# Fewer score products and paced dummies in the first four attention pairs, and units 16 to 23 computed by pairs

## The chip, the cores and the metric

The kernel runs on one core of a Trainium2 chip. The metric is the device time of one execution in microseconds (us): the median of several runs of the same program. The engines are TensorE (PE; its weight loads stand apart as PEld), VectorE (DVE), ScalarE (ACT), GpSimd (POOL) and SyncE (SP), which here only issues DMA transfers. Each engine works through its own instructions in order, and waits on semaphores for what the others make.

## The reference, cut to what matters

q, k and v are float32; the weights come as 8-byte floats, whose words the kernel converts. First an attention over 2 batches, 8 heads, 768 positions and 64 dimensions, then two feed-forward stages over 1536 tokens:

```
k_sum = k.reshape(B, H, nb, 32, D).max(axis=3)      # 24 blocks of 32 keys
v_sum = v.reshape(B, H, nb, 32, D).mean(axis=3)
scores_l = scale * q @ k.T, kept where |i - j| < 16
scores_s = scale * q @ k_sum.T + log(32)
a = softmax(concat(scores_l, scores_s))
x = a @ concat(v, v_sum)                             # to 1536 x 512
x = ((x @ w_a) * (x @ w_b)) @ w_out                  # d_ff 1536
h = x @ w_in;  out = (h - tanh(h)) @ w_out2          # d_ff 2048
```

## The kernel before, in words

**Attention.** A unit is 64 query positions of one batch; there are 24, and units 2m and 2m+1 make pair m. A unit sees a window of 96 keys (KW) and the 24 block maxima, so it has 120 score columns (NK). All products of the attention are float32, which PE runs in two passes, so that one product shows as two records. Heads go by two: p counts four couples (NP), h is the head in the couple and picks 64 of the 128 partitions.

A pair's steps are: T1, four transposes of q (`T1t`) and their copy out of PSUM (`T1e`); T2, the score products (`T2m`), then on DVE the masked scores with their maximum (`tt`), on ACT the exponentials with their sum (`ex`), on DVE the reciprocal of the sum (`rb`) and the scaling (`nm`); T3, transposes of the weights (`T3t`) and their copy (`T3e`); T4, the products with v (`T4m`), whose high half ACT writes to X (`T4h`) and whose low half DVE subtracts (`T4l`). `W` copies the 96 keys of a unit beside its 24 maxima; `q_of`, `kw_of` and `vw_of` name the buffers.

`T2m` (line 252) works on products of 64 by 64: for each p, h and unit n one. For pairs 4 and up the keys lie beside their maxima, and one product makes all 120 columns. For pairs 0 to 3 the keys are read where they are, so there are two products, one of 96 and one of 24 columns: 32 products for such a pair.

**The feed-forward stages** take tokens in three blocks of 512. Their work is a list of positions (`pos`, line 505): for each f a projection with w_a, one with w_b (`pos_a`, `pos_b`, 12 products each) and one with w_out (`pos_o`, 12 products into four accumulators). Values and weights are split into a high and a low part in fp32r, hence three products for each. Positions 0 to 35 are block 0, 36 to 70 block 1, then comes block 2, which needs X of units 16 to 23, and from about 380 us on the second stage (`pos_h`, `pos_o2`).

**The order.** Up to position 35 it is written out by hand: the list `SEQ` (line 857) names every operation in order, on all engines, under manual scheduling (line 858). Its operations go by name and number: `T2m2` is the score products of pair 2, `Mp0_0` the first products of position 0, `L` something is a load, `da` to `df` convert weights, `KP` transposes keys of batch 1, `va` adds halves of v on POOL, `vm` is the mean of v over blocks on PE (line 776), `vme` its copy by ACT (line 780), `vc` copies of it into the v buffers of the units. `tt`, `ex`, `rb`, `nm` and `T3` count halves of pairs, 2m + h. `Zu` calls `single` (line 295): two memsets and four selects on POOL that prepare masks and a zeroed q buffer for units 16 to 23.

PE gets dummies in the head. `FILL` (line 623) puts plain transposes before an operation. `PACED` (line 625) puts groups before one: each is a product that reads a softmax sum, `SM[u]` (so PE waits there until that sum is done), and six transposes that nobody reads:

```
SM, PACED = {}, {'T1t4': [0, 3, 2, 6, 5], 'T2m2': [1], 'T3t1': [4], 'T3t6': [7]}
```

From position 36 on a planner (`plan`, line 546) puts operations ahead of positions, and the framework's scheduler orders all engines but SP from position 36 to 71, by priority; what runs under `high_priority` counts as 200 instructions earlier. There units 16 to 23 are computed one by one, one every four positions: `unit_T1` (line 302) writes the q of a pair block-diagonally, so that a unit's two heads share a product, `unit_T2m` (line 314) makes four products of 128 by 128 a unit, `unit_T3` four transposes, `unit_T4` eight products. A unit's chain from T1 to T4 is up to seven positions long, so the chains of neighbours overlap. All of them run under raised priority (line 594), PE's part too. `load_q` and `load_v` are issued by SP.

Of the kernel before, what the change touches and what calls it, by code (L numbers as in the profile page):

```python
# [39 lines left out]
def band_attention_moe_kernel(ctx: ExitStack, tc: tile.TileContext, q, k, v, w_a, w_b, w_out, w_in, w_out2, out):  # L40
# [873 lines left out]
```

## Time and profile before

| | |
|---|---|
| median of 3 runs | 646.63 us (645.88 to 648.36) |
| the profiled execution | 646.71 us |
| its span, first to last instruction | 644.8 us |
| mean granted clock of TensorE | 0.997 of full |
| first projection (position 0) | 47.51 us |
| PE busy | 633.3 us, 98% |
| DVE, ACT, POOL busy | 493.6, 471.4, 194.7 us |

The profile is of one execution. Times in rows count from the first instruction of the span. A timeline row gives the start, the busy time, the engine, the line of the kernel, the operation, what it writes and reads, and in brackets how long the engine was idle before it and what ended that. The chain of waits follows the work that ended last back to the start: each piece released the next. "issue" is time in which an engine waited for nothing that the profile shows. A window row gives for one stretch the busy time of each engine with the number of its instructions, the share of TensorE's full clock that was granted, the share of DMA and its rate.

### The profile page before, as it was taken

The numbers are of one execution on the slowest core, as the hardware profiler recorded it, in microseconds if no ns is written. First come the engines' busy times: TensorE is split into PE (matmuls) and PEld (weight loads), VectorE is DVE, ScalarE is ACT, GpSimd is POOL, SyncE is SP. The second block draws the span as 40 slices with busy tenths as digits, with TensorE's granted clock in tenths as the row PEclk, the third lists the DMA queues.
The fourth block names the chain that finished last, engine by engine and source line by source line (L and its number), as shares of the span: only waits on it lengthen the run. The fifth ranks groups of instructions, "written<-read, shape, count | busy, mean of one in ns | idle before, by whom it ended". The sixth has DMA issues, their size and how long they took to land.

```text
span 644.8 us, 10213 instructions
## 1 busy us (share of the span) xinstructions
PE 633.3 (98%) x3562; PEld 516.9 (80%) x3562; DVE 493.6 (77%) x995; ACT 471.4 (73%) x994; POOL 194.7 (30%) x207
## 2 busy tenths in 40 slices
PE   7889999999999999999999999999999999999997
PEld 5578888788888887888888888888888888888885
DVE  4799999899868666458877748877777877777775
ACT  4879999997778766356555458777777777777774
POOL 3551331111101010001111144544445554444441
PEclk9899999999999999999999999999999999999999
DMA  9989997662733553023445000000010000100001
GB/s 201 274 210 265 261 232 214 190 179 71 220 111 111 170 147 100 14 101 99 146 147 163 17 1 2 0 2 1 0 67 0 2 0 1 61 6 1 1 1 65
DMA packets 81679, 62.15 MB, mean 96 GB/s; under 512 B 45716, under 2 KB 72340, under 8 KB 81628
## 3 DMA queue, kind: packets, MB, share of 16 engines
q1 hardware_dynamic: 79276, 60.32, 33.5%
q0 software_dynamic: 2352, 1.18, 1.5%
q8 instruction: 28, 0.46, 0.3%
q14 instruction: 23, 0.19, 0.1%
HBM read 54.00 MB, written 7.34 MB: 95 GB/s over the span
## 4 chain that ended last, share of the span: by engine, by line
PE 96%; DVE 1%; DMA 1%; SPq 1%; issue 0%; ACT 0%; DVEq 0%; ACTq 0%
PE acc L485 20%; PE pa L396 15%; PE pb L396 15%; PE acc L424 10%; PE acc L831 5%; PE pb L837 5%; PE pa L837 5%; PE ps L396 5%; PE pt L396 5%; PE ps L318 1%; DMA XB<-in_k_dram 1%; PE ps L366 1%; PE pt L272 1%; SPq L642 1%; PE ps L631 1%; PE pt L356 1%
## 5 line engine op out<-in xcount | busy, mean ns | idle before, releaser
L185 POOL TENSOR_TENSOR wsp<-w,wsp 128x512 fp32r<-128x512 f32 x97 | 127.7, 1335 | 139.8 <-ACT wsp L184 139.8
L184 ACT ACTIVATE wsp<-w 128x512 fp32r<-128x512 f32 x165 | 98.8, 621 | 13.4 <-PE acc L424 9.4
L179 POOL TENSOR_SCALAR w<-w 128x512 f32<-128x512 f32 x39 | 26.5, 682 | 185.7 <-ACT w L154 97.3
L485 PE MATMUL acc<-wsp,gh 128*128 128x512 f32 x256 | 78.9, 389 | 0.0
L185 DVE TENSOR_TENSOR wsp<-w,wsp 128x512 fp32r<-128x512 f32 x68 | 48.4, 713 | 36.5 <-ACT wsp L184 36.2
L424 PE MATMUL acc<-gh,wsp 128*128 128x512 f32 x192 | 63.5, 391 | 0.0
L396 PE MATMUL pb<-XB,wsp 128*128 128x512 f32 x240 | 60.5, 394 | 0.0
L396 PE MATMUL pa<-XB,wsp 128*128 128x512 f32 x240 | 60.0, 394 | 0.0
L389 ACT ACTIVATE gh<-tg 128x512 fp32r<-128x512 f32 x56 | 34.9, 623 | 30.0 <-DVE tg L412 29.7
L485 PEld LDWEIGHTS acc<-wsp,gh 128*128 128x128 f32 x256 | 48.1, 188 | 10.0
L396 PEld LDWEIGHTS pa<-XB,wsp 128*128 128x128 f32 x240 | 44.5, 188 | 9.5
L396 PEld LDWEIGHTS pb<-XB,wsp 128*128 128x128 f32 x240 | 44.4, 188 | 9.1
L485 PE MATMUL acc<-wsp,gl 128*128 128x512 f32 x128 | 49.8, 389 | 0.0
L485 PE MATMUL acc<-wsp,vw 128*128 128x512 f32 x192 | 46.5, 390 | 0.0
L396 PE MATMUL pa<-XA,wsp 128*128 128x512 f32 x192 | 46.1, 389 | 0.0
L396 PE MATMUL pb<-XA,wsp 128*128 128x512 f32 x192 | 46.1, 389 | 0.0
L390 DVE TENSOR_TENSOR gl<-tg,gh 128x512 fp32r<-128x512 f32 x56 | 38.5, 687 | 8.8 <-ACT gh L389 8.8
L485 PEld LDWEIGHTS acc<-wsp,vw 128*128 128x128 f32 x192 | 35.9, 188 | 8.2 <-ACT vw L389 0.4
L396 PEld LDWEIGHTS pb<-XA,wsp 128*128 128x128 f32 x192 | 36.0, 188 | 7.5
L396 PEld LDWEIGHTS pa<-XA,wsp 128*128 128x128 f32 x192 | 36.0, 188 | 7.5
L424 PEld LDWEIGHTS acc<-gh,wsp 128*128 128x128 f32 x192 | 35.9, 188 | 7.3
L837 PE MATMUL pa<-XA,wsp 128*128 128x512 f32 x144 | 37.3, 398 | 0.6 <-DVE XA L767 0.6
(332 smaller groups left out, 1442.7 us busy)
## 6 DMA issues: line engine op xcount, KB each, us to landing
stage<-in_moe_w_out_dram SPq DMA_DIRECT2D x19, 512.0 KB, 3.5
stage<-in_moe_w_in_dram SPq DMA_DIRECT2D x16, 512.0 KB, 4.6
stage<-in_moe_w_a_dram SPq DMA_DIRECT2D x8, 512.0 KB, 5.4
w<-wsc SPq DMA_DIRECT2D x16, 256.0 KB, 3.7
vw<-in_v_dram SPq DMA_DIRECT2D x19, 192.0 KB, 4.8
stage<-in_moe_w_b_dram SPq DMA_DIRECT2D x7, 512.0 KB, 4.5
wsc<-x21a SPq DMA_DIRECT2D x8, 256.0 KB, 4.5
wsc<-x21b SPq DMA_DIRECT2D x8, 256.0 KB, 4.8
```

The costliest lines, as they stand in the source:

```text
L179: eng.tensor_scalar(rf, rf, HI_HI, HI_LO, op0=ALU.min, op1=ALU.max)
L184: nc.scalar.activation(s[:, 0, :], r, AF.Copy)
L185: eng.tensor_tensor(s[:, 1, :], r, s[:, 0, :].bitcast(F32), op=ALU.subtract)
L272: mm(pp[h][n * 64 : n * 64 + 64, p, c0:c1], qt[r, p, n * 64 : n * 64 + 64], keys[r, p, :], start=True, stop=True,)
L318: mm(pp[:, p, 0:NK], qt[:, p, :], kw[:, p, :], start=True, stop=True)
L389: nc.scalar.activation(dst[0], src, AF.Copy)
L390: eng.tensor_tensor(dst[1], src, dst[0].bitcast(F32), op=ALU.subtract)
L396: mm(dst, w, xx, start=(kk == 0 and n == 0), stop=(kk == KC - 1 and n == 2))
L424: mm(acc[blk][d][:, c0:c1], w, t, start=(f == 0 and c0 == 0 and n == 0), stop=(f == F1 - 1 and n == 2))
L485: mm(a[c], g[:, cs], s[:, i, :], start=(f == 0 and n == 0), stop=(f == F2 - 1 and n == 2))
L831: mm(acc[0][c], w, t, start=(f == 0 and m == 0), stop=(f == F1 - 1 and m == 2))
L837: mm(P_["M", i], w, t, start=(c == 0 and m == 0), stop=(c == KC - 1 and m == 2))
```

## The change

For pairs 0 to 3, `T2m` makes the 96-column products first, for all p; then for each p and h one product of 24 columns for both units at once, with 128 output rows: 16 + 8 products instead of 16 + 16. `PACED` keeps one group, on sum 6 before `T1t4`; seven are gone. Units 16 to 23 go by pairs 8 to 11, with `T1`, `T2`, `T2b`, `T3` and `T4` in place of the `unit_` functions: q is no longer block-diagonal, scores come from `T2m` into two banks, and T4 from `T4m`. Pair m's chain starts eight positions after that of the pair before and ends before the next one's scores: T1 one position ahead of T2 (two for the first), T3 five behind, T4 seven behind. T1, T3 and T4 raise only the copies out of PSUM in priority and T2 its softmax; the products on PE stay at the priority of their position. `load_q` and two `load_v` are issued once a pair. `single` and `Zu` go. Masks come from `mask_of`. SEQ is otherwise the same.

```diff
--- before.py
+++ after.py
@@ -81,17 +81,6 @@
     kq = xb[:, 0:3072].rearrange("p (c h d) -> p c h d", c=NC, h=H)
     qbx = xb[:, 3072:4096].rearrange("p (u x c) -> p u x c", u=2, x=NP)
 
-    def band_mask(m, h, off):
-        band = m[h * 64 : h * 64 + 64, 0:KW]
-        nc.gpsimd.affine_select(
-            out=band, in_=band, pattern=[[1, KW]], compare_op=ALU.is_gt, fill=NEG,
-            base=WIN - off, channel_multiplier=-1,
-        )
-        nc.gpsimd.affine_select(
-            out=band, in_=band, pattern=[[-1, KW]], compare_op=ALU.is_gt, fill=NEG,
-            base=WIN + off, channel_multiplier=1,
-        )
-
     def constants():
         nc.vector.memset(bsq, -math.sqrt(GA) * GB)
         nc.vector.memset(bth, -GC2)
@@ -110,7 +99,15 @@
             nc.gpsimd.memset(m[:, 0:KW], 0.0)
             nc.gpsimd.memset(m[:, KW:NK], math.log(BLK) / SC)
             for h, off in enumerate(offs):
-                band_mask(m, h, off)
+                band = m[h * 64 : h * 64 + 64, 0:KW]
+                nc.gpsimd.affine_select(
+                    out=band, in_=band, pattern=[[1, KW]], compare_op=ALU.is_gt, fill=NEG,
+                    base=WIN - off, channel_multiplier=-1,
+                )
+                nc.gpsimd.affine_select(
+                    out=band, in_=band, pattern=[[-1, KW]], compare_op=ALU.is_gt, fill=NEG,
+                    base=WIN + off, channel_multiplier=1,
+                )
 
 
     def unit_src(u):
@@ -244,6 +241,17 @@
     def q_of(m):
         return qbx[:, m - 2] if m in (2, 3) else qbd[:, m % 2]
 
+    def soon():
+        return tc.high_priority(offset=HP)
+
+    def T1(m, tag):
+        t = qn.pop(m)
+        pp = pt(tag, (128, NP, 128))
+        for p in range(NP):
+            nc.tensor.transpose(pp[:, p, :], t[:, 2 * p : 2 * p + 2, :], ident)
+        with soon():
+            nc.scalar.activation(q_of(m), pp, AF.Copy)
+
     def W(u):
         b, w, k0 = where(u)
         kw = kw_of(u)
@@ -263,7 +271,7 @@
                 if m > 3:
                     parts.append(((0, NK, kw_of(2 * m + n)),))
                 else:
-                    parts.append(((0, KW, kt[b][:, :, k0 : k0 + KW]), (KW, NK, kt[b][:, :, S : S + NB])))
+                    parts.append(((0, KW, kt[b][:, :, k0 : k0 + KW]),))
             for i in range(len(parts[0])):
                 for h in range(2):
                     r = slice(h * 64, h * 64 + 64)
@@ -273,11 +281,58 @@
                             pp[h][n * 64 : n * 64 + 64, p, c0:c1], qt[r, p, n * 64 : n * 64 + 64], keys[r, p, :],
                             start=True, stop=True,
                         )
+        if m < 4:
+            for p in range(NP):
+                for h in range(2):
+                    r = slice(h * 64, h * 64 + 64)
+                    mm(pp[h][:, p, KW:NK], qt[r, p, :], kt[b][r, p, S : S + NB], start=True, stop=True)
         for h in range(2):
             at_x[m, h] = pp[h]
 
     def mask_of(m):
         return masks[0 if m % (S // 128) == 0 else (2 if m % (S // 128) == S // 128 - 1 else 1)]
+
+    def T2s(m, h):
+        pp = at_x[m, h]
+        e = st([128, NP, NK], "e", 2)
+        nm = st([128, NP], "nm", 8)
+        sm = st([128, NP], "sm", 8)
+        for p in range(NP):
+            nc.vector.tensor_tensor_reduce(
+                out=e[:, p, :], in0=pp[:, p, 0:NK], in1=mask_of(m), scale=-SC, scalar=3.0e38,
+                op0=ALU.add, op1=ALU.min, accum_out=nm[:, p : p + 1],
+            )
+            nc.scalar.activation(
+                e[:, p, :], e[:, p, :], AF.Exp, scale=-1.0, bias=nm[:, p : p + 1], accum_out=sm[:, p : p + 1]
+            )
+        at_x[m, h] = (e, sm)
+
+    def T2(m, tags):
+        T2m(m, tags)
+        with soon():
+            for h in range(2):
+                T2s(m, h)
+
+    def T2b(m, h):
+        e, sm = at_x[m, h]
+        nc.vector.tensor_scalar(sm, sm, 1e-9, None, op0=ALU.add)
+        nc.vector.reciprocal(sm, sm)
+        if h:
+            nc.vector.tensor_tensor(e, e, sm.unsqueeze(2).to_broadcast([128, NP, NK]), op=ALU.mult)
+        else:
+            for p in range(NP):
+                nc.scalar.activation(e[:, p, :], e[:, p, :], AF.Copy, scale=sm[:, p : p + 1])
+        at_x[m, h] = e
+
+    def T3(m, h, tag):
+        e = at_x.pop((m, h))
+        pp = pt(tag, (128, NP, 128))
+        for p in range(NP):
+            nc.tensor.transpose(pp[0:NK, p, :], e[:, p, :], ident)
+        at = st([NK, NP, 128], "at", 2)
+        with soon():
+            nc.scalar.activation(at, pp[0:NK], AF.Copy)
+        at_x[m, h] = at
 
     def T4m(m, tag, n=None):
         at = [at_x.pop((m, h)) for h in range(2)]
@@ -292,86 +347,14 @@
                     mm(pp[h * 64 : (h + 1) * 64, p, c], vt[:, 2 * p + h, :], at[h][:, p, c], start=True, stop=True)
         return pp
 
-    def single():
-
-        nc.gpsimd.memset(qbd, 0.0)
-        nc.gpsimd.memset(masks[0][:, 0:KW], 0.0)
-        for h in range(2):
-            band_mask(masks[0], h, 2 * WIN)
-
-    def unit_T1(m, tag, qt):
-        t = qn.pop(m)
-        pp = pt(tag, (128, NP, 128))
-        for p in range(NP):
-            nc.tensor.transpose(pp[:, p, :], t[:, 2 * p : 2 * p + 2, :], ident)
-        for h in range(2):
-            r = slice(h * 64, h * 64 + 64)
-            dst = qt[r, :, :, h * 64 : h * 64 + 64]
-            nc.scalar.activation(dst, pp[r].rearrange("x p (u c) -> x u p c", u=2), AF.Copy)
-        for r in range(2):
-            qb[2 * m + r] = qt[:, r]
-
-    def unit_T2m(u, tag):
-        qt, kw = qb.pop(u), kw_of(u)
-        pp = pt(tag, (128, NP, 128))
-        for p in range(NP):
-            mm(pp[:, p, 0:NK], qt[:, p, :], kw[:, p, :], start=True, stop=True)
-        at_x[u] = pp
-
-    def unit_T2s(u):
-        pp = at_x[u]
-        e = st([128, NP, NK], "e", 2)
-        nm = st([128, NP], "nm", 8)
-        sm = st([128, NP], "sm", 8)
-        mk = masks[0 if u == 2 * (S // 64) - 1 else 1]
-        for p in range(NP):
-            nc.vector.tensor_tensor_reduce(
-                out=e[:, p, :], in0=pp[:, p, 0:NK], in1=mk, scale=-SC, scalar=3.0e38,
-                op0=ALU.add, op1=ALU.min, accum_out=nm[:, p : p + 1],
+    def T4(m, tag):
+        pp = T4m(m, tag)
+        x, c0 = X[m // 4], (m % 4) * 128
+        with soon():
+            nc.scalar.activation(x[:, 0, :, c0 : c0 + 128], pp, AF.Copy)
+            nc.vector.tensor_tensor(
+                x[:, 1, :, c0 : c0 + 128], pp, x[:, 0, :, c0 : c0 + 128].bitcast(F32), op=ALU.subtract
             )
-            nc.scalar.activation(
-                e[:, p, :], e[:, p, :], AF.Exp, scale=-1.0, bias=nm[:, p : p + 1], accum_out=sm[:, p : p + 1]
-            )
-        at_x[u] = (e, sm)
-
-    def unit_T2(u, tag):
-        unit_T2m(u, tag)
-        unit_T2s(u)
-
-    def unit_T2b(u):
-        e, sm = at_x[u]
-        nc.vector.tensor_scalar(sm, sm, 1e-9, None, op0=ALU.add)
-        nc.vector.reciprocal(sm, sm)
-        if u % 2:
-            nc.vector.tensor_tensor(e, e, sm.unsqueeze(2).to_broadcast([128, NP, NK]), op=ALU.mult)
-        else:
-            for p in range(NP):
-                nc.scalar.activation(e[:, p, :], e[:, p, :], AF.Copy, scale=sm[:, p : p + 1])
-        at_x[u] = e
-
-    def unit_T3(u, tag):
-        e = at_x.pop(u)
-        pp = pt(tag, (128, NP, 128))
-        for p in range(NP):
-            nc.tensor.transpose(pp[0:NK, p, :], e[:, p, :], ident)
-        at = st([NK, NP, 128], "at", 2)
-        nc.scalar.activation(at, pp[0:NK], AF.Copy)
-        at_x[u] = at
-
-    def unit_T4(u, tag):
-        at, vt = at_x.pop(u), vw_of(u)
-        pp = pt(tag)
-        for p in range(NP):
-            for h in range(2):
-                mm(
-                    pp[h * 64 : (h + 1) * 64, p * 64 : (p + 1) * 64], vt[:, 2 * p + h, :], at[:, p, h * 64 : (h + 1) * 64],
-                    start=True, stop=True,
-                )
-        x = X[u // 8]
-        c0 = (u % 8) * 64
-        src = pp[:, 0:256].rearrange("x (p c) -> x p c", p=NP)
-        nc.scalar.activation(x[:, 0, :, c0 : c0 + 64], src, AF.Copy)
-        nc.vector.tensor_tensor(x[:, 1, :, c0 : c0 + 64], src, x[:, 0, :, c0 : c0 + 64].bitcast(F32), op=ALU.subtract)
 
     xtag = ["XA", "XB"]
 
@@ -565,24 +548,23 @@
 
 
     OFF = -2
-    for n, u in enumerate(range(16, 24)):
-        j = max(n * 4 + begin[1] + OFF, HEAD_P)
-        b, w, _ = where(u)
-        if u % 2 == 0:
-            m = u // 2
-            if m + 2 < 12:
-                plan(j, load_q, m + 2)
-            plan(j, unit_T1, m, "pt", qbd)
-            plan(j, W, u)
-            plan(j, W, u + 1)
-        if u % 8 == 0:
-            plan(j, new_x, u // 8)
-        plan(j + 2, unit_T2, u, "ps")
-        plan(j + 3, unit_T2b, u)
-        plan(j + 5, unit_T3, u, "pt")
-        plan(j + 7, unit_T4, u, "ps")
-        if u + 3 < 24:
-            plan(j + 7, load_v, u + 3)
+    for n, m in enumerate(range(8, 12)):
+        j = HEAD_P + 8 * n + 2
+        plan(j - 1 - (n == 0), T1, m, "pt")
+        plan(j, T2, m, ("ps", "pt"))
+        if m + 2 < 12:
+            plan(j, load_q, m + 2)
+        for h in range(2):
+            plan(j + 1, T2b, m, h)
+            plan(j + 5, T3, m, h, ("pt", "ps")[h])
+        for u in (2 * m, 2 * m + 1):
+            plan(max(j - 4, HEAD_P), W, u)
+        if m % 4 == 0:
+            plan(j, new_x, m // 4)
+        plan(j + 7, T4, m, "ps")
+        for u in (2 * m + 3, 2 * m + 4):
+            if u < 24:
+                plan(j + 7, load_v, u)
     for d in range(KC):
         plan(begin[2] + 4 * d + 4, split_x2, 0, d)
         plan(begin[3] + 4 * d + 8, split_x2, 1, d)
@@ -591,7 +573,7 @@
 
     def run_plan(j):
         for fn, args in at.pop(j, ()):
-            if fn in (unit_T1, unit_T2, unit_T2b, unit_T3, unit_T4, W) and HP:
+            if fn in (T2b, W):
                 with tc.high_priority(offset=HP):
                     fn(*args)
             else:
@@ -622,7 +604,7 @@
     P_A, P_B = ([j for j in range(HEAD_P) if pos[j][0] is fn] for fn in (pos_a, pos_b))
     FILL = {'KP1': 1, 'T1t0': 5, 'T1t1': 5}
 
-    SM, PACED = {}, {'T1t4': [0, 3, 2, 6, 5], 'T2m2': [1], 'T3t1': [4], 'T3t6': [7]}
+    SM, PACED = {}, {'T1t4': [6]}
 
     def warm(n, d):
         for u in PACED.get(n, ()):
@@ -647,8 +629,6 @@
                 vp["q"] = st([128, 2, H, D], "x20" + "ab"[i // 2])
             qn[i] = vp["q"][:, i % 2]
             nc.sync.dma_start(qn[i], q[0, :, i * 128 : (i + 1) * 128, :].rearrange("h p d -> p h d"))
-        elif k == "Zu":
-            single()
         elif k == "LV":
             load_v(i)
         elif k == "Lv":
@@ -854,7 +834,7 @@
         else:
             raise Exception(n)
 
-    SEQ = '... Mt11 sh37 Zu Mp34_0 Lw38 ...'
+    SEQ = '... Mt11 sh37 Mp34_0 Lw38 ...'
     with tc.manual_schedule():
         nc.vector.memset(qbd, 0.0)
         for _ in range(WARM):
```

## Rows read from the trace of the kernel before

**Rows 1.** The page: busy time of engines; the chain by engine.
```profile
PE 633.3 (98%) x3562; PEld 516.9 (80%) x3562; DVE 493.6 (77%) x995; ACT 471.4 (73%) x994; POOL 194.7 (30%) x207
...
PE 96%; DVE 1%; DMA 1%; SPq 1%; issue 0%; ACT 0%; DVEq 0%; ACTq 0%
```

**Rows 2.** Chain of waits, 16 to 48 us: start us, us, what.
```profile
18.07 1.94 issue
...
24.61 2.77 PE pb L776 x6
...
36.96 0.44 PE acc L752 x4
...
45.66 1.81 DVE XA L767 x3
```

**Rows 3.** Windows: busy PE, PEld, DVE, ACT, POOL; clock, DMA, GB/s.
```profile
20.00:21.00 1.00, 0.99 (x28) 0.94 (x28) 0.02 (x1) 1.00 (x7) 1.00 (x1) 0.64 1.10 344
...
23.00:24.00 1.00, 1.00 (x39) 1.00 (x41) 0.00 (x0) 0.00 (x0) 0.80 (x1) 0.65 1.09 354
```

**Rows 4.** Timeline of DVE in the head: start us, us, instruction, idle before.
```profile
24.69 0.28 DVE L723 CUSTOM_DVE_ANT_0 tg<-pa,mask 128x120 f32<-128x120 f32 x1 [2.00 <-PE pa L272]
...
29.20 1.10 DVE L620 COPY w<-w 24x512 f32<-24x512 f32 x1
...
35.86 0.65 DVE L745 TENSOR_TENSOR tg<-tg,sm 128x480 f32<-128x480 f32 x1
```

**Rows 5.** Window of the planned stretch, columns as in rows 3.
```profile
163.00:260.00 97.00, 96.88 (x572) 78.92 (x571) 69.11 (x168) 69.53 (x166) 9.67 (x14) 1.00 0.47 137
```

**Rows 6.** Chain of waits, 174 to 192 us: one unit's products.
```profile
176.15 0.88 PE ps L318 x8
...
179.77 2.72 PE acc L424 x12
182.49 0.62 PE ps L366 x16
```

**Rows 7.** Chain of waits, 100 to 115 us: pair 6's T2m, a T4m.
```profile
104.54 0.25 PE ps L272 x2
...
105.53 2.28 PE pb L837 x9
...
111.20 1.08 PE ps L292 x32
```

**Rows 8.** SyncE's queue waits, 130 to 270 us: total, times, longest.
```profile
SPq L237 <- PE ps L366: 38.3, 5, 10.0
```

**Rows 9.** Waits of ACT, 163 to 260 us: total, times, longest.
```profile
ACT stage L155 <- DMA stage<-in_moe_w_in_dram: 14.2, 10, 2.8
```

**Rows 10.** Timeline of PE in the head: T2m's steps, dummies.
```profile
13.53 0.28 PE L272 MATMUL pt<-kt,qbd 64*64 64x96 f32 x2
...
13.72 0.19 PE L272 MATMUL pt<-kt,qbd 64*64 64x24 f32 x2
...
13.81 0.28 PE L272 MATMUL pt<-kt,qbd 64*64 64x96 f32 x2
...
27.31 0.38 PE L629 MATMUL ps<-ident,sm 128*4 128x128 f32 x2
27.62 0.88 PE L631 MATMUL ps<-ident 128*128 128x128 f32 x6
28.42 0.38 PE L629 MATMUL ps<-ident,sm 128*4 128x128 f32 x2
```

**Rows 11.** Timeline of GpSimd in the head.
```profile
21.58 1.27 POOL L771 TENSOR_TENSOR XA<-XA 128x512 f32<-128x512 f32 x1 [0.53 <-DMA XA<-in_v_dram]
```

**Rows 12.** Timeline of ACT in the head.
```profile
27.41 0.59 ACT L780 ACTIVATE w<-pb 24x512 f32<-24x512 f32 x1 [0.22 <-PE pb L776]
...
33.50 0.60 ACT L618 ACTIVATE qbd<-ps 128x512 f32<-128x512 f32 x1 [1.21 <-PE ps L699]
...
38.30 0.60 ACT L618 ACTIVATE gl<-pt 120x512 f32<-120x512 f32 x1 [2.58 <-PE pt L752]
```

More of the change, by code (lines that the diff above doesn't have):

```diff
@@ new lines, in band_attention_moe_kernel @@
+    SEQ = 'LK0 LK1 LK2 LK3 LK4 LK5 Lq0 Lq1 Lq2 Lq3 Lv0 Lv1 Lv2 Kt0 Kr0 Kt1 Kt2 Kr1 Kt3 Kt4 Kt5 T1t0 Lw0 Ke0 Ke1 Kr3 Ke2 va0 Lw1 Kr2 Ke4 Ke5 Kr4 Ke3 Kr5 W9 T1t1 T1e0 T1e1 T2m0 Lw2 W11 tt1 tt0 W8 T2m1 va1 Lw3 T1t3 W10 T1t2 Lq4 T1e3 ex1 tt3 rb1 ex0 ex3 T2m3 T1e2 va2 T2m2 tt2 ex2 tt6 tt7 vm tt5 Lk0 rb0 ex6 tt4 rb3 rb2 nm3 ex5 rb6 da1 rb5 nm2 vme ex4 vc1 T1t4 LV0 dc1 da0 dd1 da2 nm6 ex7 vc5 de1 dc2 nm1 LV1 LV2 rb4 T3t2 T1e4 dc0 nm4 nm0 dd0 T3t0 T3t3 T3t1 db0 rb7 LV3 LV4 de0 nm7 T3t4 nm5 da3 LV5 T3t5 LV6 dc3 vc2 T3t6 T3e3 T3e5 T3e2 dd2 vc3 LV7 T3t7 dd3 vc4 Lk1 T3e1 de2 T3e0 db1 df0 T3e4 de3 vc7 KP0 vc0 KE0 db2 vc6 KR0 T3e7 T4m1 T4h1 T4l1 Lw4 db3 Lw5 df3 df1 T3e6 df2 T4m0 T4m2 T2m4 sh1 Lw6 T4h2 tt8 T4m3 sl1 sh0 sl0 T4h0 Lw7 KP1 T4h3 da4 da5 T4l2 Lw8 Lk2 db4 T4l0 T4l3 Mp0_0 sh2 da6 KR1 dc4 Mp0_1 Mp0_2 sh3 Mp0_3 Mp1_0 KE1 Ma0 dc5 dd4 dd5 Mp1_1 sl2 Mp1_2 LV8 db7 db5 da7 Mp1_3 Mp2_0 de5 LV9 sl3 da8 dc7 dc6 Mp2_1 de4 dd6 Mp2_2 Lk3 db6 Lq5 df4 tt9 Mt0 sh4 df5 Mp2_3 Lw9 db8 Mp3_0 de6 dc8 Mh0 Mp3_1 W12 Mp3_2 dd7 sl4 Mp3_3 dd8 Ml0 Mp4_0 sh5 df6 Lk4 ex9 sl5 Mp4_1 ex8 Ma1 de8 db9 da9 de7 Mp4_2 rb9 Mp4_3 df7 df8 Mp5_0 sh7 sh6 dc9 Mt1 sh8 LV10 KP2 rb8 Mp5_1 Mp5_2 dd9 Mp5_3 Lw10 Mh1 sl6 sl7 Mp6_0 KE2 de9 da10 Lw11 Mp6_1 dc10 KR2 Lw12 df9 dd10 KP3 KP4 db10 da11 Mp6_2 Mp6_3 nm9 Lw13 KE3 Ml1 Mp7_0 sl8 da12 Mp7_1 de10 Ma2 KR3 dc12 dc11 db11 KR4 Lq6 nm8 dd11 da13 Lk5 df10 sh9 Mp7_2 Mp7_3 de11 sh10 dc13 Mt2 Mp8_0 LA0 T1t5 sl9 Lw14 df11 Mp8_1 T1e5 dd12 Mh2 KE4 db12 sh11 dd13 de12 Mp8_2 Mp8_3 Ma3 de13 sl10 Mp9_0 db13 df12 Ml2 Mp9_1 T3t8 df13 T3t9 db14 Mp9_2 sl11 Mp9_3 Lw15 Lw16 T3e8 sh12 Lq7 T3e9 Mp10_0 sl12 sh13 sl13 da15 Mp10_1 da14 da16 Mt3 dc14 Lw17 LA1 db16 db15 dc15 T2m5 Mp10_2 Mp10_3 Mp11_0 tt10 dd14 dd15 ex10 dc16 Mp11_1 de14 Lw18 Mp11_2 da17 de15 Mh3 LA2 df14 tt11 sh14 Lw19 Mp11_3 Mp12_0 dd16 Ma4 Mp12_1 Ml3 db17 Lq8 Mp12_2 dc17 df15 Mp12_3 de16 dd17 W13 rb10 ex11 df16 sl14 sh15 sl15 Mp13_0 KP5 da18 db18 KR5 sh16 de17 Mp13_1 da19 Mp13_2 KE5 rb11 dc18 Mt4 Mp13_3 V12 db19 Mp14_0 Mh4 nm10 Lw20 Lw21 dd18 df17 dc19 dd19 da20 Mp14_1 Mp14_2 Lq9 de18 Mp14_3 Mp15_0 de19 Lw22 sh17 db21 Ma5 T4m4 Mp15_1 Ml4 T4h4 sl16 Mp15_2 LA3 Mp15_3 df18 sh18 Mp16_0 df19 sl17 Lw23 da21 T1t6 db20 sh19 Mp16_1 Mp16_2 Mp16_3 T1e6 sl18 nm11 Mt5 da22 T4l4 Mp17_0 Mh5 dc21 V13 T3t10 dc20 dd21 sl19 T3e10 Mp17_1 dd20 T3t11 Mp17_2 Mp17_3 db22 de21 dc22 Lw24 de20 dd22 df20 LV11 T3e11 db23 Ml5 sh20 df21 Mp18_0 T2m6 Ma6 Lw25 de22 Lw26 Mp18_1 Mp18_2 da23 da24 sl20 dc23 sh21 tt12 ex12 Mp18_3 tt13 Mp19_0 db24 ex13 df22 Lw27 da25 dd23 Mp19_1 Mp19_2 Mp19_3 Mp20_0 db25 Mt6 de23 dc24 dd24 T4m5 sh22 Mh6 Mp20_1 sl21 T4h5 Mp20_2 LV12 Mp20_3 da26 df23 dc25 Mp21_0 db26 de24 dd25 T1t7 Mp21_1 Ml6 rb12 Mp21_2 da27 db27 sl22 Mp21_3 df24 dc26 Mp22_0 T4l5 de25 nm12 Lw28 T3t12 LV13 T1e7 dd26 df25 dc27 mv0 rb13 mv1 Mp22_1 Lw29 de26 LV14 sh23 sh24 nm13 T3e12 W15 sh25 Mp22_2 Ma7 dd27 sl23 de27 T3t13 Lw30 df26 mvE W14 da28 df27 Mt7 Mp22_3 Mp23_0 dc28 LM12 dd28 T3e13 T2m7 db28 sl24 sh26 Mp23_1 da29 Mh7 tt14 de28 tt15 Mp23_2 sl25 da30 ex14 Mp23_3 Mp24_0 Ma8 Mp24_1 LM13 Mp24_2 rb14 sh27 T4m6 df28 Lw31 LM14 Mp24_3 Ml7 Mp25_0 nm14 sl26 dc29 Mp25_1 Mp25_2 dd29 ex15 db30 dc30 rb15 dd30 Lw32 sl27 T4h6 da31 nm15 Mp25_3 LV15 da32 db29 Mt8 T4l6 de29 Mp26_0 T3t14 de30 T3t15 Mp26_1 db32 Mp26_2 dc31 df29 T3e14 dd31 T3e15 dc32 T4m7 LV16 Mh8 sh28 df30 Ml8 T4h7 Mp26_3 de31 T4l7 Mp27_0 Lw33 db31 db33 Mp27_1 sh29 Lw34 sl28 Mp27_2 dd32 df31 Mp27_3 Mp28_0 sl29 Lw35 sh30 da33 Ma9 da34 Mp28_1 da35 sl30 LV17 de32 db34 LV18 Mt9 dc33 dc35 dd33 db35 dd35 Mp28_2 Mp28_3 de35 sh31 Mp29_0 Mh9 df32 sh32 Mp29_1 Mp29_2 Mp29_3 Mp30_0 Mp30_1 de33 sl31 Mp30_2 Ml9 df33 Ma10 Mp30_3 Mp31_0 sl32 dc34 Mt10 dd34 de34 df34 Mp31_1 Mp31_2 Lw36 df35 Mp31_3 sh33 Mp32_0 Mh10 Mp32_1 Mp32_2 sl33 Ml10 sh34 sl34 Mp32_3 Lw37 sh36 Ma11 sh35 Mp33_0 sl36 sl35 Mp33_1 Mp33_2 Mp33_3 Mt11 sh37 Mp34_0 Lw38 sl37 Mh11 Mp34_1 Mp34_2 Mp34_3 Ml11 sh38 Mp35_0 sl38 Mp35_1 Mp35_2 Mp35_3 XE1 XE0 XE2 XE3'
```

1 line of the change is left out of this document (removed).

## Prediction

> **What bounds the kernel now.** I read the page first. TensorE (PE) is busy 98% of the span, and the chain that ended last runs over PE for 96% of it [rows 1]. So a change is worth what it takes off PE, or off what PE waits for, and nothing else. The profiled execution took 646.71 us: its span of 644.8 and 1.9 around it. That is 0.1 above the median of the runs, 646.63, so I sum against 646.71 and carry the result over as it is. What a measurement can tell from no change is 0.5%, here 3.2 us.
>
> Then I asked where the two touched stretches lie. The first is the head, before the first projection at 47.5 us. There PE is not the bound by its own work: in the chain of waits its pieces stand between pieces of VectorE (DVE) and ScalarE (ACT) [rows 2], and the reader should look for three things. One: PE starts nothing for 1.94 us from 18.07, a gap that the profile gives to "issue", that is to nothing it can see [rows 2]. Two: right behind the gap the granted clock is at the lower of its two levels, 1.2 instead of 2.4 GHz, from about 20.3 to 23.7, while PE works: a stretch of 3.4 us [rows 3]. Three: DVE then runs from 24.69 to 47.47 with hardly a gap, and its last piece, the low halves of X [rows 2], releases the first projection. It began that run 2.00 us late, waiting for the fourth score product, T2m2 [rows 4].
>
> The second stretch is the planned one, 163 to 260 us, in which units 16 to 23 lie between projections. PE is busy 96.88 of 97 us in it, at full clock [rows 5]. There a microsecond of PE is a microsecond of the kernel.
>
> **Units by pairs.** Transposes stay as many (T1 four a pair, T3 eight). The scores were one block-diagonal product of 0.88 us a unit [rows 6], 8 x 0.88 = 7.04. They become T2m, which pairs 4 to 7 already use: between other work it takes from 104.54 to 105.53, 0.99 [rows 7], 4 x 0.99 = 3.96. That is 3.1 less. T4 was 0.62 a unit [rows 6], 4.96 in all; as T4m it is 1.08 a pair [rows 7], 4.32: 0.6 less. Sum of the pairs: 3.7 us less, all on the path.
>
> T2m stands there with its 64x64 products between projections of 128x128. Its first step takes 0.25, the other seven 0.74 together, so about 0.11 each [rows 7]: a change of shape costs some 0.14, and the 0.99 holds it.
> The Trainium skill ("TensorEngine Tiling (Array Packing)", Key Properties) says that a change of tiling mode, unlike a change of tile, drains the engine, which speaks against products in quarters; the trace agrees, as the first step shows, and by rule and row the sum is the same, because the drain is inside the row that I multiply.
>
> The rest is off the path. ACT copies q once at full height instead of twice at half height, DVE and ACT write X four times instead of eight; softmax is as before. The cover is that no row of this stretch has PE waiting for either; without it, the links priced under the rivals count. The loads of v go out two at a time behind T4 instead of one by one, and SyncE stands before them until T4 is done, with the weight loads queued behind: that wait was 38.3 us in five pieces before, up to 10.0, and ACT waited 14.2 us for weight loads, without a wait on PE [rows 8, 9]. I take 0. Zu (two memsets, four selects) leaves GpSimd, busy 30% [rows 1]: 0. PE's own pieces lose their raised priority while the evacuations keep it; this moves them, and costs only through those links.
>
> **Score products of the first four pairs.** A step of T2m (eight products) takes 0.28: 0.19 for the 96-column part, 0.09 for the four of 24 columns, from 13.72 to 13.81 [rows 10]. Those four become two with 128 output columns; no row has that shape. If the two cost nothing, a T2m gains 4 x 0.09 = 0.36; if as much as two 96-column ones, 0.19 / 2, it loses 0.02. I take half of the four, 0.045, since the columns streamed are the same 24: 0.18 a T2m. It only brings products forward that wait for DVE or for v afterwards, so I add nothing.
>
> **Dummies.** A paced group (two products on a softmax sum, six transposes) takes 1.11, from 27.31 to 28.42 at full clock [rows 10]. Eight groups become one. The one before T2m2 goes, and with it the wait for its sum. T2m3 and T2m2 then end near 21, whether the 1.94 us gap stays, shrinks or moves behind fewer instructions: DVE's 2.00 us wait goes either way, since DVE has softmax work until 22.7. But what comes next is vm, the mean of v. It cannot start before GpSimd has added the last v, 21.58 + 1.27 = 22.85 [rows 11]. It takes 2.77 at full clock, from 24.61 to 27.38 [rows 2]. With PE almost idle from 18 to 22.9, the lower clock is likely at its start. If the stretch at half clock is as long again as in rows 3, vm does 3.7 of its six steps in them and ends at 22.85 + 3.4 + 2.3 x 0.46 = 27.3: where it ended before. Bounds: 25.6 at full clock, 28.4 at half throughout. I take 27.4.
>
> Behind vm, ACT copies it (0.59), and DVE's copy L620 at 29.20 needs that [rows 4, 12]. It can go at 28.05: DVE is 1.15 early from there on. ACT waited 1.21 us for T1t4 behind five groups, now one, and 2.58 us for T3t5, which sat behind the group on sum 4 [rows 12]. T3t4 waits for DVE's product of 35.86 [rows 4], now 1.15 earlier; T3t4 and T3t5 at 0.44 each [rows 2], or 0.88 at half clock, let ACT go on at about 37.2 instead of 38.30, 1.1 early. PE is through with what precedes T3t4 at 27.4 + 1.1 + 5 x 0.44 = 30.7 and idles for 4.6 us, so I count the half clock, and 0.2 more for the transposes behind it. The head gains 0.9 us. Ends: 2.9 less, if vm ends at 25.6 and DVE's copy goes at 26.3; 1.7 more, from rival one with vm at 28.4.
>
> Sum: 646.71 - 3.7 - 0.9 = **642.1 us**.
>
> **Rivals.** *The clock takes the head's gain.* The dummies kept PE at 2.4 GHz from 23.7 on. Without them it is idle twice, about 2 and 4.6 us; after 1.94 us the clock fell [rows 2, 3]. If 3.4 us of T3, KP0 and T4m run at half speed, PE ends them 1.7 us later; with 1.0 gained before, the head is 0.7 longer: 646.7 + 0.7 - 3.7 = 643.7, which counts as no change. Against it: DVE's own queue sets the end there, and has PE idle beside it.
> The Trainium skill ("TensorE: Matmul & The Clock Gate", HAM oscillation — how this bites in real kernels) holds that idle stretches of PE return it to the lower clock; the half-rate stretch of rows 3 agrees, and by it this rival's 643.7 would stand where the forecast has 642.1.
>
> *The head gains all*, with vm at full clock: 2.9 less, 640.1. For it: the gap of 1.94 may vanish. Against it: PE has little to do before 22.85 in any case.
>
> *The pairs wait.* T1 lies one position (2.72 us of PE [rows 6]) ahead of T2m, where priority let it run far ahead before. If ACT stands in front of T1's copy waiting for a weight load, up to 2.8 [rows 9], then with two pieces of ACT of 0.6 each [rows 12] that is 4.0, and PE waits 1.3; in the same way T4's evacuation holds the next T2m in its bank, with T1 and a position between (0.44 + 2.72), 0.8. Four pairs: 8.4 us, 650.5, slower. It decides from 1.95 us a pair (7.8 in all); about 1 us a pair gives 646, no change. Against it: ten such waits in 97 us make 14.2, and mostly ACT runs.
>
> *Quarters are no cheaper than whole products* between fp32r projections, so that only T4 gains: 645.2. Against it: rows 7.
>
> **How the numbers follow.** Forecast 0.50; clock 0.17; all of the head 0.11; pairs slower 0.10; pairs waiting a little 0.07; quarters 0.05. Faster by over 0.5% (below 643.4) are the forecast and the full head: 0.61. Within 0.5%: clock, little waits, quarters: 0.29. Slower by over 0.5%: the waiting pairs, 0.10. The range reaches from 639.6 (full head, with products at their better bound) to 646.2 (pairs waiting a little); outside are the slower case and the far tails, under 0.2.
>
> **What would show it.** Right: no single-unit products left, T2m four times at about 1.0 and T4m at 1.1 in a stretch that ends 3.7 sooner against its begin; PE idle there under 0.5; in the head DVE without its 2.0 us wait, vm ending between 27 and 28 at half clock, ACT's 2.58 wait shorter, and the first projection at 46.6. Wrong: PE idle before T2m or T4m; a first projection at or past 47.5 with the clock at half behind 35; T2m far from 1.0; or a new "issue" gap.

## The result, and the profile after

The changed kernel takes **641.37 us** (median of 6 runs, 640.48 to 643.63) against 646.44 for the kernel before beside it (6 runs, 644.36 to 648.36): a ratio of 0.9917, with a 95% interval from 0.9899 to 0.9935. That is 5.1 us less; 4.6 had been predicted.

The profiled execution is the longest of the six, 643.63 us, with a mean granted clock of 0.989; the others had 0.995 to 0.997. Its page, busy time and the chain by engine, answers to [rows 1]:

```profile
PE 628.9 (98%) x3506; PEld 513.0 (80%) x3506; DVE 491.4 (77%) x991; ACT 467.9 (73%) x986; POOL 192.9 (30%) x201
...
PE 96%; DVE 2%; DMA 1%; SPq 1%; issue 0%; ACT 0%
```

PE is still the bound and has 4.4 us less to do. The head shows in the chain of waits of the same execution, 16 to 48 us (start, us, what), beside [rows 2]:

```profile
23.84 4.67 PE pb L756 x6
28.52 0.60 ACT w L760
29.15 0.42 DVE w L602
...
35.94 1.08 PE ps L732 x4
...
40.43 3.34 PE acc L347 x96
...
45.78 1.81 DVE XA L747 x3
```

The "issue" gap of 1.94 us is gone. But vm (L756) takes 4.67 us instead of 2.77, ends at 28.5, and the low halves of X (L747) end where they ended before. The first projection starts at 47.64; before it was 47.51. (In every kernel its very first product stands about a microsecond earlier, since it needs only the high half of X; the times here are those of the second.) In this execution the head gave nothing. The windows of that stretch say why (busy time of PE, PEld, DVE, ACT and POOL, then the granted clock), beside [rows 3]:

```profile
21.00:27.00 6.00, 6.00 (x48) 3.93 (x41) 4.96 (x43) 5.05 (x25) 3.20 (x3) 0.50 1.14 321
28.00:34.00 6.00, 3.79 (x30) 2.91 (x28) 5.12 (x8) 5.42 (x21) 5.55 (x7) 1.00 1.26 189
35.00:41.00 6.00, 5.06 (x32) 4.76 (x34) 5.87 (x14) 3.74 (x9) 0.34 (x1) 0.50 0.84 182
```

PE ran at 1.2 GHz from 21 to 27 us, and again from 35 to 41, after it had been idle for 2.2 of the 6 us from 28 to 34 and then until 35.94. That is rival one. A second profile of the same kernel, the execution of 641.10 us of e11 below, shows another head. Its chain:

```profile
34.57 1.08 PE ps L732 x4
...
43.35 1.81 DVE XA L747 x3
45.21 2.79 PE pa L817 x11
```

and its windows:

```profile
21.00:27.00 6.00, 4.21 (x26) 2.17 (x25) 5.83 (x40) 5.95 (x29) 3.51 (x4) 1.00 1.14 321
28.00:34.00 6.00, 2.40 (x20) 2.16 (x20) 5.87 (x11) 4.27 (x14) 4.60 (x6) 1.00 1.11 208
35.00:37.00 2.00, 2.00 (x12) 2.00 (x11) 2.00 (x6) 0.46 (x1) 0.00 (x0) 0.50 1.29 215
```

Same program: at full clock vm needs 2.83 us and is no longer in the chain, which runs over DVE up to T3t4 at 34.57 instead of 35.94; the low clock behind 35 is over by 37.6 instead of 41, and the first projection starts at 45.21, 2.4 sooner than in the other execution. One kernel has several heads.

In the planned stretch, the chain of the profiled execution shows the new pieces: a T4m and a T1, and pair 9's T2m, which takes its place from 198.62 to 199.60 (its first three pieces), beside [rows 6, 7]:

```profile
191.91 1.08 PE ps L347 x32
193.00 0.59 PE pt L251 x4
193.59 2.76 PE pb L379 x12
...
198.62 0.24 PE pt L280
198.86 0.01 PE ps L280 x2
198.87 0.09 PE pt L280 x2
```

Pair 8's T2m is not in one piece. It lies in three among the projections, from 150.79, 157.24 and 171.00. Here is the middle one:

```profile
156.79 0.45 PE pb L817 x2
157.24 0.24 PE pt L280
...
157.60 0.01 PE pt L280
157.61 2.51 PE pb L817 x10
```

What a piece of attention adds is read from the gap between the start of the projection product ahead of it and the start of the one behind, less 0.227, a product's own step (2.72 for twelve). By that, T2m adds 1.07 for each of pairs 9 to 11, and 0.66 + 0.46 + 0.64 = 1.76 for pair 8. Its two breaks cost 0.69, a third of a whole T2m each.

### The profile page after: what moved, and what is told of

It reads as the page before. It is cut to its first block, busy times and chain, and to the rows that moved or that the text cites. A ratio compares the mean times of both kernels' runs of the same rounds, so it can differ in the third digit from the quotient of the medians.

```text
span 641.7 us, 10069 instructions
## 1 busy us (share of the span) xinstructions
PE 628.9 (98%) x3506; PEld 513.0 (80%) x3506; DVE 491.4 (77%) x991; ACT 467.9 (73%) x986; POOL 192.9 (30%) x201
## 4 chain that ended last, share of the span: by engine, by line
PE 96%; DVE 2%; DMA 1%; SPq 1%; issue 0%; ACT 0%
PE acc L468 20%; PE pa L379 15%; PE pb L379 15%; PE acc L407 10%; PE pb L817 5%; PE pa L817 5%; PE acc L811 5%; PE pt L379 5%; PE ps L379 5%; PE ps L347 1%; PE pt L280 1%; DMA XB<-in_k_dram 1%; PE pb L756 1%; SPq L624 1%; PE acc L347 1%; PE ps L732 1%
## 5 line engine op out<-in xcount | busy, mean ns | idle before, releaser
L379 PE MATMUL pb<-XB,wsp 128*128 128x512 f32 x240 | 59.1, 392 | 0.0
```

What stands on the lines that cost most here:

```text
L379: mm(dst, w, xx, start=(kk == 0 and n == 0), stop=(kk == KC - 1 and n == 2))
```

## The experiments

All were timed beside the kernel before, whose median was 646.0 us (17 runs) beside e1 to e4, 646.12 (11) beside e5 to e8 and 646.5 (23) beside e9 to e11. First, each half of the change alone.

**e1_pairs_only**: new pairs, head as before.

```diff
-                    parts.append(((0, KW, kt[b][:, :, k0 : k0 + KW]),))
+                    parts.append(((0, KW, kt[b][:, :, k0 : k0 + KW]), (KW, NK, kt[b][:, :, S : S + NB])))
...
-    SM, PACED = {}, {'T1t4': [6]}
+    SM, PACED = {}, {'T1t4': [0, 3, 2, 6, 5], 'T2m2': [1], 'T3t1': [4], 'T3t6': [7]}
```

(the separate 24-column products go as well)

> The new pairs, with the old score products and all eight groups of dummies. Theory (the pairs bring about 3.2 us, the head the remaining 1.9 of the median's 5.1): 643.2 us, the first projection near 47.5 as before. Rival one (the pairs bring nearly all, as the changed kernel's profile with its first projection at 47.6 would have it): 641.4. Rival two (the prediction's own sum, 3.7): 642.7.

Measured: 641.93 us (641.51 to 643.77, 6 runs), ratio 0.9929 [0.9902, 0.9956].

**e2_head_only**: the kernel before with the new products and one paced group.

```diff
-                    parts.append(((0, KW, kt[b][:, :, k0 : k0 + KW]), (KW, NK, kt[b][:, :, S : S + NB])))
+                    parts.append(((0, KW, kt[b][:, :, k0 : k0 + KW]),))
...
+        if m < 4:
+            for p in range(NP):
+                for h in range(2):
+                    r = slice(h * 64, h * 64 + 64)
+                    mm(pp[h][:, p, KW:NK], qt[r, p, :], kt[b][r, p, S : S + NB], start=True, stop=True)
...
-    SM, PACED = {}, {'T1t4': [0, 3, 2, 6, 5], 'T2m2': [1], 'T3t1': [4], 'T3t6': [7]}
+    SM, PACED = {}, {'T1t4': [6]}
```

> The new score products and the one group of dummies, with units 16 to 23 one by one. Theory: 1.9 us less than before, 644.5. Rival one (the head brings nothing): 646.4. Rival two (the prediction's head, 0.9): 645.5. Planned stretch as before: 0.81 us a unit for scores, 0.71 for the products with v.

Measured: 645.38 us (644.83 to 646.95, 12 runs), ratio 0.9986 [0.9971, 1.0002].

**e3_old_products**: the changed kernel with 16 + 16 products again (the first part of e1's diff alone).

> The changed kernel with the old 16 + 16 score products for pairs 0 to 3. Theory (the products of 24 columns and 128 output columns cost 0.22 us a step against 0.09, so that T2m takes 1.8 instead of 1.1, and this lies ahead of DVE): about 1 us less than the changed kernel, 640.4. Rival (fewer products help by up to 0.2 each, or hide): 641.4 to 642.

Measured: 641.94 us (641.40 to 644.61, 6 runs), ratio 0.9933 [0.9907, 0.9959].

**e4_old_dummies**: the changed kernel with all eight paced groups (the second part of e1's diff alone).

> The changed kernel with all eight groups of dummies. Theory (taking seven groups out is worth 2 to 3 us, the clock's loss included): 643.5 to 644.5. Rival (the lower clock gives all of it back): 641.4, or less, with full clock from 24 us on and the first projection at 47.6 or earlier.

Measured: 642.02 us (641.83 to 642.91, 6 runs), ratio 0.9929 [0.9906, 0.9952].

By the medians the pairs make 4.0 to 4.1 of the 5.1 us (the changed kernel against e2, e1 against before). The head's edits bring 0.6 together (e2), and leaving out either one costs the same 0.6 (e3, e4), which these runs can't tell from nothing. By the medians, then, the theories of e1 and e2 (3.2 for the pairs, 1.9 for the head) fell, and e2 lies at its rival two, the prediction's own 0.9. The theories of e3 (640.4) and e4 (643.5 to 644.5) missed as well; e3 lies in its rival's range and e4 0.6 above its own. The traces divide the gain otherwise:

| kernel | products, groups | gap "issue" | first projection | from there to the end |
|---|---|---|---|---|
| before | old, 8 | 1.94 | 47.51 | 597.2 |
| e1 | old, 8 | 2.14 | 47.61 | 594.0 |
| e2 | new, 1 | none | 46.08 | 598.1 |
| e3 | old, 1 | 2.31 | 45.93 | 593.9 |
| e4 | new, 8 | none | 46.08 | 593.9 |
| changed, first profile | new, 1 | none | 47.64 | 594.1 |
| changed, second profile | new, 1 | none | 45.21 | 593.9 |

From the first projection on, each kernel with pairs in this table takes 3.2 to 3.3 less than the kernel before (e5 and e7, below, 2.8 less). That is what the pairs are worth. e2 takes 0.9 more there: PE waited twice for 0.4 at a T3 of its units, once for ACT and once for DVE, where the changed kernel has no such wait. The rest lies in the head. There e3 and e4 have the first projection 1.5 to 1.7 sooner than e1; but e1's profile is of an execution of 643.60 us, 1.7 over e1's median, so this does not show what an edit is worth. Executions differ, and each one's mean granted clock is known; here they stand by it (number, mean us). In the profiles of these kernels the clock is full from 47.7 us on, so there what the mean lacks was lost in the head:

| kernel | 0.999 or 1 | 0.996 to 0.998 | 0.994 or 0.995 | 0.993 or less |
|---|---|---|---|---|
| before, all 51 | 13, 645.0 | 25, 646.5 | 7, 647.7 | 6, 648.9 |
| e1 | 4, 641.7 | 2, 643.7 | | |
| e4 | 6, 642.1 | | | |
| e3 | | 1, 641.4 | 3, 641.9 | 2, 643.7 |
| changed, 12 with e11 | | 7, 641.0 | 4, 642.3 | 1, 643.6 |

Along each row the time climbs by 0.5 to 2 us a column. At a like clock the changed kernel is 5.3 to 5.5 under the one before, e1 2.8 to 3.3. So e1's 4.1 was probably in part luck, four of six executions at full clock where the kernel before, with the same head, had 13 of 51. At a like clock the head would be worth some 2.3, of which the changed kernel gives part back, since none of its executions kept the full clock; but the clock is itself something that the edits change. On the mean of 646.55 before, less 3.2 for the pairs, 643.3 would be left; the changed kernel's mean is 641.63. By this estimate the head's net gain is about 1.7. No run shows it bare: e2 is under the kernel before by 0.6 at the medians and 0.9 at the means, having lost 0.9 in its two waits, and the changed kernel is under e1 by 0.6 and 0.7, with e1's full clocks.

Next, what the products cost, and whether a steady clock would bring more.

**e5_quarters_last**: the 24-column products in quarters of 64 outputs, still behind the others.

```diff
-                    mm(pp[h][:, p, KW:NK], qt[r, p, :], kt[b][r, p, S : S + NB], start=True, stop=True)
+                    for n in range(2):
+                        mm(
+                            pp[h][n * 64 : n * 64 + 64, p, KW:NK], qt[r, p, n * 64 : n * 64 + 64],
+                            kt[b][r, p, S : S + NB], start=True, stop=True,
+                        )
```

> The changed kernel with the 24-column products of pairs 0 to 3 still behind the others, but each as two 64x64 quarters again (16 for 8). Theory (a 24-column product onto 128 outputs costs PE more than two quarters, since its weights take 188 ns against 133 ns to load): the first pair's score products take 1.1 to 1.2 us instead of 1.82. Rival (it is their place behind the others): they stay at 1.7 to 1.9. In the total both expect no more than 0.5 us from the changed kernel (641.4), since the first pairs' products lie beside other work.

Measured: 641.7 us (640.86 to 642.25, 5 runs). Timeline of PE, the changed kernel's first T2m (its first product, two of the 24-column ones, and the next T2m's first), start and busy us:

```profile
13.04 0.30 PE L280 MATMUL pt<-kt,qbd 64*64 64x96 f32 x2
...
13.99 0.27 PE L288 MATMUL pt<-kt,qbd 64*128 64x24 f32 x1
...
14.10 0.27 PE L288 MATMUL pt<-kt,qbd 64*128 64x24 f32 x1
...
14.86 0.30 PE L280 MATMUL pb<-kt,qbd 64*64 64x96 f32 x2
```

and e5's:

```profile
13.12 0.30 PE L280 MATMUL pt<-kt,qbd 64*64 64x96 f32 x2
...
13.87 0.22 PE L289 MATMUL pt<-kt,qbd 64*64 64x24 f32 x2
...
13.92 0.22 PE L289 MATMUL pt<-kt,qbd 64*64 64x24 f32 x2
...
14.27 0.28 PE L280 MATMUL pb<-kt,qbd 64*64 64x96 f32 x2
```

A T2m takes 1.82 us in the changed kernel (13.04 to 14.86), 1.15 in e5, and 1.12 before. A pair of new products steps by 0.11, two passes make 0.22 a p; the quarters step by 0.055, 0.11 a p. The theory holds in that it is the shape, not the place. That the weight loads set the price fits their durations in the first T2m (ns: least, median, largest):

```profile
L280 PEld LDWEIGHTS pt<-kt,qbd x16: 129/133/133, 13.0 to 13.6; 64*64 64x64 f32 x16
...
L288 PEld LDWEIGHTS pt<-kt,qbd x8: 183/188/188, 13.9 to 14.6; 64*128 64x128 f32 x8
```

And in the total it does not show: e5 is 0.3 over the changed kernel. Fewer products cost PE 0.67 us more a T2m, beside other work.

e5 also has the "issue" gap again:

```profile
20.09 0.24 PE L289 MATMUL ps<-kt,XB 64*64 64x24 f32 x2 [2.13 <-issue]
```

**e6_warm_idle**: old products, one group, and plain transposes where PE idles. **e7_warm_new**: new products, one more group and transposes.

```diff
-    FILL = {'KP1': 1, 'T1t0': 5, 'T1t1': 5}
+    FILL = {'KP1': 1, 'T1t0': 5, 'T1t1': 5, 'T3t1': 24}
...
-    SM, PACED = {}, {'T1t4': [6]}
+    SM, PACED = {}, {'T1t4': [6], 'T2m2': [1]}
```

(this is e7; e6 has e3's products and `'T2m3': 6, 'T2m2': 10, 'T3t1': 24` in `FILL`)

> The changed kernel with the old products of pairs 0 to 3 and one paced dummy group, and plain transposes where PE idles behind pairs 2 and 3 and the first T3 (6, 10 and 24 of them). Theory (the clock of the first 45 us sets whether the head gains): full clock from 20 us on, the first projection at 45.0 to 45.6, 640.0 to 641.0 us. Rival (the head hangs on transfers and on VectorE, whatever the clock): first projection at 45.9 to 46.5, 641.5 to 642.3. A third (the transposes stand in the path): first projection at 47 and 642.5 or more.

> The changed kernel with its new products, one more paced dummy group (behind pair 2) and 24 plain transposes behind the first T3. Theory (clock): full clock from 24 us on, PE's wait of 4.15 us ahead of the gates' transposes down to 2 or less, first projection at 45.0 to 45.9, 640.0 to 641.0 us, and less spread over the executions than 640.5 to 643.6. Rival (transfers and VectorE): 641.2 to 642, spread as before.

Measured: e6 642.33 us (641.16 to 643.97, 6 runs), e7 641.47 (640.98 to 642.03, 5 runs). Both profiles have full clock throughout and the first projection at 45.44 and 45.03. In e7 all five executions had 0.997 or more and lie within 1.05 us; e6's clock still fell in four of six. So e7 bears out the theory's smaller spread, but both theories' times, 640.0 to 641.0, missed, and the rivals' hold: a full clock bought with dummies is no faster than the changed kernel's median. From 45.03 on e7 needed 594.4, not 594.0, and the transposes stand in PE's queue too.

Then the one loss in the planned stretch: pair 8's T2m in three pieces.

**e8_first_whole**: it gets the raised priority.

```diff
-        T2m(m, tags)
+        if m == 8:
+            with soon():
+                T2m(m, tags)
+        else:
+            T2m(m, tags)
```

> The changed kernel with the score products of pair 8 given the raised priority, so that they stand in one piece instead of three among the projections. Theory (each break into another kind of product costs PE 0.2 to 0.35 us): the pair's score products add 1.07 us instead of 0.66 + 0.46 + 0.64 = 1.76, the time falls by 0.7, to 640.7. Rival (the softmax that starts on them is late at the pair's T3, now nearer behind): 0.2 to 0.7 of a wait there, 641.2 to 641.6.

Measured: 643.04 us (642.78 to 644.09, 5 runs). T2m adds 1.07, as wanted, and the kernel is 1.7 longer than the changed one. The chain:

```profile
166.39 5.04 DMA stage<-in_moe_w_in_dram
...
172.20 0.53 ACT wsp L181
...
173.36 0.68 DVE x21b L161
174.04 0.61 DVE tg L399
...
174.70 3.06 PE pb L383 x12
```

PE waited 1.57 us for the gate product (tg), which stands in DVE's queue behind the conversion of a weight block that came late. The value products fell into pieces of 20, 2 and 10 instead, 0.65 us more (by the same gaps). Neither theory nor rival had named that wait.

**e9_both_whole**: T4m of pair 8 raised too. **e10_whole_warm**: the same with e7's dummies. **e11_changed_again**: the changed kernel.

```diff
-        pp = T4m(m, tag)
+        with soon() if m == 8 else ExitStack():
+            pp = T4m(m, tag)
```

> The changed kernel with the score products and the value products of pair 8 both given the raised priority, so that neither is broken (in the run before, only the score products had it, the value products then fell into pieces of 20, 2 and 10, and PE waited 1.57 us for VectorE's gate product behind a late weight block). Theory (each break costs PE 0.2 to 0.35 us, and the wait came of the pair's chain being moved between the weight blocks): score products 1.07 instead of 1.76 in three pieces, value products 1.2 in one, no wait over 0.3, 640.7 us. Rival (PE is then ahead of the weight stream at 170 us, whatever is broken): a wait for VectorE's gate product of 1.5 to 2.3 us there again, 642.3 to 643.0.

> The kernel of the run above with one more paced dummy group behind pair 2 and 24 plain transposes behind the first T3, which kept TensorE at 2.4 GHz from 20 us on in an earlier run. By the theory 640.6 to 640.9 with little spread; by the rival 642.3 to 643.0. If the head's clock decides the spread from execution to execution, the clocks of all executions are 0.997 or more and the times lie within 1.2 us.

> The changed kernel itself, beside the others on the same chip: 641.4, between 640.5 and 643.6. If the clock of the head makes its spread, its longest executions are those of the lowest mean clock.

Measured: e9 645.80 us (643.68 to 647.53, 12 runs), e10 643.83 (643.36 to 646.43, 12 runs), e11 641.47 (640.78 to 642.63, 6 runs). e11's three executions at 0.996 or 0.997 are its three shortest, as expected. In e9 no T2m or T4m is broken any more, and it is the worst of all. PE's waits, 160 to 270 us:

```profile
PE pa L384 <- ACT ta L392: 2.0, 1, 2.0
PE pb L384 <- DVE tg L400: 0.6, 1, 0.6
```

The first is at 208.47. ACT's timeline ahead of it shows the copy (ta, L392) that empties PE's bank behind the softmax of pair 9:

```profile
200.67 0.68 ACT L152 ACTIVATE stage<-stage 128x512 int32<-128x512 uint32 x1 [1.61 <-DMA stage<-in_moe_w_in_dram]
...
203.15 0.38 ACT L305 ACTIVATE e<-e,nm 128x120 f32<-128x120 f32 x1
...
206.70 1.24 ACT L328 ACTIVATE e<-e,sm 128x120 f32<-128x120 f32 x4
207.84 0.57 ACT L392 ACTIVATE ta<-pa 128x512 f32<-128x512 f32 x1
```

ACT stood 1.61 us for a weight block, then did eight exponentials and the scaling, and the bank was free 2.0 us late. The wait has an echo, in the windows of e9:

```profile
200.00:208.00 8.00, 6.47 (x29) 5.03 (x27) 6.61 (x29) 7.33 (x27) 1.17 (x1) 1.00 0.06 22
209.00:212.00 3.00, 3.00 (x8) 2.34 (x7) 2.90 (x5) 1.61 (x3) 0.00 (x0) 0.50 0.03 5
```

PE fell to 1.2 GHz right after, in a stretch that runs at full clock in every kernel without that wait. The Trainium skill ("TensorE: Matmul & The Clock Gate", HAM oscillation) says that waits of PE for transfers throw it back to the lower clock; here PE waited for ACT, which had waited for a transfer, and the trace agrees, 0.50 behind a wait of 2.0. From the first projection on, e9's profile needs 597.8 us, 3.9 more than the changed kernel's. In e9 both the theory's 640.7 and the rival's 642.3 to 643.0 fell; e10, with clocks from 0.994 to 1.0 and 3.1 us between its executions, missed what was expected of its spread too. Its profile, of an execution of 645.96 us, has full clock all through the head and then the same wait, 1.9 us, with 0.50 from 209 to 212: in e9 and e10 a low mean clock can come from this stretch, not from the head. The changed kernel, with its pieces, has neither wait. No version beats it.

## Why the prediction was right, point by point

**The sign and the size** are right: 4.6 forecast, 5.1 measured, 641.4 inside 639.6 to 646.2. The two halves are off in opposite directions, whichever way the gain is divided (3.2 and about 1.7 by the traces and means, 4.1 and 0.6 by the medians, for 3.7 and 0.9), and make up for each other. That the sum came within 0.5 us is in part luck.

**The pairs, 3.7 forecast, measured 3.2** (597.24 to 594.08 in the two profiles; 593.9 in e3, e4 and e11, 594.4 and 594.5 in e7 and e5). The sums of the gaps between projection starts, 130 to 300 us, divide it. T2 went from 6.65 for eight units to 4.97 for four pairs: 1.7 less, where 3.1 was forecast. A unit adds 0.81 in most cases, not the 0.88 of [rows 6], and a T2m 1.07 whole and 1.76 broken, not the 0.99 of [rows 7]. The step that failed is the multiplication of 0.99 by four: I took for granted that the scheduler leaves a T2m whole, and read both prices between ends, where the step into the piece is missing. T4 went from 5.74 to 4.86: 0.9 less, where 0.6 was forecast. What is left, about 0.6, lies by 0.1 in the T3 and by the rest between projection products with no piece of attention between them; for it I had nothing, and its cause stays open.

**Everything off the path** was hidden as argued. PE has no wait from 163 to 260 us, where it is busy 97.00 of 97. SyncE's wait before the loads of v is 36.4 us in four pieces, and ACT waited 11.1 us for weight loads, without a wait on PE [rows 8, 9]. The slower rival, waiting pairs, did not come about. But e8 and e9 show that its mechanism is near: a pair's chain moved by some positions gives waits of 1.6 and 2.0 us.

**The score products** were counted at nothing, and that holds in the total: they lie in the head beside other work, and the 0.67 us that each T2m lost does not show in e5. My bounds for the new shape, 0 to 0.095 a p, were wrong: 0.22. I had bounded it by columns streamed; by e5 it goes with the width of the weights. The lower end of the range, 639.6, takes 0.5 off the full head's 640.1 for the better of these bounds, a figure that the prediction does not work out. With the new products the gap of [rows 2] is gone (below). What that is worth is not shown: with all eight groups and full clock the old products (e1) take 641.7 and the new ones (e4) 642.1, and e5, which has the gap, is 0.3 over the changed kernel.

**The head, 0.9 forecast, about 1.7 estimated on the mean, 0.6 at the medians.** Of its steps, vm's end at 27.4 lay between the ends that occurred, 28.5 in the first profile (bound 28.4) and 24.6 in the second (bound 25.6). That second bound was wrong by a microsecond: it let vm start only behind GpSimd's last addition, at 22.85, but vm is three products and only the last reads that part of v. In the second profile vm starts at 21.80, while the addition lasts until 22.62. In the first it starts late, at 23.84, since T2m2, put at "near 21", ended there at half clock. DVE's 2.00 us wait for T2m2 went down to 0.93 in the first and away in the second. PE's wait for the product ahead of T3t4 is 4.15 and 3.53, for 4.6 forecast. Rival one, the clock taking the head's gain, is what the first profile shows: the first projection at 47.64 and the low clock behind 35 are what the prediction had named as a sign of being wrong. The second profile has the low clock behind 35 too, for 2.6 us, and the gain all the same, and the mean clocks of the others, 0.994 and up against 0.989, speak against rival one there. The step that failed is to give one number to a quantity that differs from execution to execution.

## What to carry to other kernels

Where PE is the bound, price a piece of foreign shape by the starts of the products around it, and by how often it will be broken, since each break costs about as much as a third of the piece. Before moving a chain for such a fraction, see what stands in the in-order queues between it and late transfers: 0.7 us saved on PE cost 1.7 and 4.4. And compare executions at a like granted clock: here executions of one kernel lie 1 to 2 us apart with the clock of the first 45 us, as much as the edits under test. A kernel with another head has another mix of clocks, so compare the means too.

## What the runs showed of the hardware

The gap in which PE waits for nothing that the profile shows is there, 1.94 to 2.31 us long, in the profiles of all five kernels with 16 + 16 score products (before, e1, e3, e5, e6) and in none of the others, whatever the dummies and the order. In the chain of e3 it reads:

```profile
18.01 2.31 issue
```

In all five it falls behind the same record of PE, the 221st of its products' records, and ends at 20.0 to 20.3 us. The kernels with the new products have started only 200 to 204 by 20 us, since theirs are fewer and longer, and reach the 222nd at 20.4 or later. The windows from 0 to 20 us show it, first before, then changed (the number behind PE's busy time):

```profile
0.00:20.00 20.00, 14.14 (x221) 10.62 (x222) 11.05 (x48) 11.92 (x40) 7.16 (x32) 1.00 1.13 220
0.00:20.00 20.00, 16.37 (x200) 12.77 (x200) 10.45 (x40) 11.58 (x38) 8.26 (x32) 1.00 1.15 223
```

What PE waits for there stays open. Either fewer instructions ahead of that point avoid the wait, or PE comes to it when the wait would be over in any case; no run here tells these apart.

A product of 24 columns onto 128 outputs steps by 0.11 us for two at once, against 0.055 for four quarters at once that stream as many columns. The step goes with the width of the weights, and half the products took twice the time.
